# A deeper staging ring for float64 weights, their low parts on VectorE, and queries and keys of eight head pairs turned on TensorE

## The chip, the cores and the metric

The kernel runs as one program on 1 core of a Trainium2 chip. The metric is the device time of one execution in microseconds (us). Three runs of the kernel before gave 1021.06, 1022.9 and 1025.08 us; the median is 1022.9 us. A difference of less than about 0.5% (5 us) can't be told from no change here.

## The reference

Three layers follow one another: blockwise causal attention, a two-layer feed-forward block whose weights come as float64, and a soft mixture of experts.

```
q, k, v: 8 batches x 8 heads x 576 x 64
scores = q @ k.T / 8, masked so that block i (64 rows) sees blocks j <= i
x  = softmax(scores) @ v                       -> 4608 tokens x 512
h  = x @ w_in   (512 x 2048, given as float64)
g  = where(h > 0, h, exp(min(h, 0)) - 1)
x  = g @ w_out  (2048 x 512, given as float64)
logits = x @ phi (32 slots);  d = softmax over tokens;  c = softmax over slots
slot_in  = d.T @ x;  slot_out[e] = relu(slot_in[e] @ w1[e]) @ w2[e]
out = c @ slot_out                             -> 4608 x 512, float32
```

## The kernel before, in words

The 64 heads are worked in 32 pairs; pair `n` has batch `n // 4`. The 4608 tokens are worked in 36 tiles of 128. A small planner (`Plan`, `add`, `order`) simulates all operations with rough durations and sorts them by a key; its result is a fixed order of instructions on each engine. The engines then run their lists in order, each instruction waiting for its semaphores. SP issues nearly all DMAs, in order too. Where the planner sees TensorE at rest, it places small bf16 matmuls that nothing reads (L994, here called fillers).

**A pair.** `pair_load` brings q and k of the pair into `RQ` and `RK` (two slots each) with eight DMAs of 72 KB: one for each tensor, head and half of the head's 64 columns. Each reads runs of 32 floats (128 bytes), 576 of them, so that 32 x 32 blocks lie where VectorE's block transpose needs them. `pair_prep` turns q and k with one VectorE transpose each (L452) and scales q on GpSimd (L454). `pair_scores` makes scores (L490, L494), their row maxima on VectorE (L503) and the exponentials on ScalarE (L506). `pair_weights` divides by the sums on GpSimd (L523), transposes the weights on TensorE (through `transpose`, L317) and copies them out of PSUM. `pair_values` multiplies by v (L589, L593).

**The float64 weights.** `w_in` and `w_out` are each read in 16 pieces of 512 KB as pairs of 32-bit words. `narrow` makes float32 of a piece: one rescaling of the high words on ScalarE or GpSimd (L375, L377), then three VectorE operations (L379, and L382 twice), from a raw buffer (`raws`, here five; GT and G are the later buffers of the tiles) into an output buffer (`outs`, here two called narrow and two called wot). `first_weights` then keeps a rounded high part (ScalarE, L392) and the rest, the low part (GpSimd, L393), for each `w_in` piece. `second_weights` stores each narrowed `w_out` piece to DRAM (`wo_f`), transposes it on TensorE (L317) and multiplies it with phi (L411, the projection) into a PSUM bank that `give_back` copies into WP. `w_in` pieces take raw buffers 0 to 4 and outputs 0 to 3 in turn; `w_out` pieces take raw buffers 3 to 5 and only the two narrow outputs, of which each stays occupied until its store to DRAM has landed.

**A tile.** `tile_range` multiplies a tile with a quarter of `w_in` (L626 to L628: high by high, high by low, low by high; four such steps for each quarter), and VectorE applies the activation. The tile is then turned by way of DRAM (`turned`), meets WP (L668) and updates the dispatch sums. Since WP and several buffers of the tiles are taken by the weight conversion, the tiles can't run steadily before the last projection (L411). From there to the tail TensorE works without gaps. The tail computes the experts and the output.

Of the kernel before, what the change touches and what calls it, by code (L numbers as in the profile page):

```python
# [14 lines left out]
AF = mybir.ActivationFunctionType  # L15
# [10 lines left out]
KWIN, KWOUT = -92.0, -42.0  # L26
KWS, KWOS, KA0, KAS, KCON, KLD, KSTAGE, NPB = 3.5, 1.0, -109.0, 14.0, -98.0, 30.0, 26.0, 4
NEV, NQ = 16, 1
TLAG, LATE = 2.5, 30
TICK, DUTY, FILL, FN = 3.4, 0.5, 0.055, 128  # L30
# [170 lines left out]
def attention_moe_kernel(ctx: ExitStack, tc, q, k, v, w_in, w_out, phi, w1, w2, consts, out):  # L201
# [129 lines left out]
    def start():  # L331
# [11 lines left out]
        def zero(e):  # L343
            for s in range(2):
                nc.gpsimd.memset(f(PB + PW[0] * s + S, 64), 0.0)
            for s in range(NV):
# [7 lines left out]
               [(GT + 1024 * j, 512, gtk(j)) for j in range(2)] + \  # L354
               [(XR + 2 * RING + S, RING, [("xr", p, 1, j) for p in (2, 3) for j in range(2)])]
        outs = [(PAD + 512 * j, ("narrow", j)) for j in range(2)] + [(C + 512 * j, ("wot", j)) for j in range(2)]

# [29 lines left out]
        def first_weights(j):  # L387
            r, kk = divmod(j, 4)
            kw = KWIN + KWS * j
            w32, wk = narrow(win32[P * kk:P * kk + P, 1024 * r:1024 * r + 1024], kw, j % 5, j % 4)  # L390
            hi, lo = W[r] + 512 * kk, W[r] + PIECE + 512 * kk
            add("ACT", 0.5, lambda e: nc.scalar.copy(fr(hi, 512), f(w32, 512)), r=[wk], w=[("wh", r, kk)], key=kw)  # L392
            add("POOL", 1.25, lambda e: nc.gpsimd.tensor_tensor(  # L393
                out=fr(lo, 512), in0=f(w32, 512), in1=f(hi, 512), op=ALU.subtract),
                r=[wk, ("wh", r, kk)], w=[("wl", r, kk)], key=kw)

        def second_weights(m):
            kw = KWOUT + KWOS * m
            w32, wk = narrow(wout32[P * m:P * m + P, :], kw, 3 + m % 3, m % 2)
            load(wo_f32[P * m:P * m + P, :], f(w32, 512), 1 << 18, r=[wk], w=[("wod", m)], key=kw)  # L400
# [14 lines left out]
        def give_back():  # L415
            add(CP2, cpdur(512), lambda e: copy(e, f(WP, 512), pb(GTB, 512)), r=["gtb"], w=["wp"], key=KWOUT)
            for j, (_, _, keys) in enumerate(raws):
                handover(keys, [("stage", j)])
            handover(["c"], [("wot", 0), ("wot", 1)])
            handover([("tt", 0, r) for r in range(2)], [("narrow", 0), ("narrow", 1)])  # L420
            handover([("e", 0), ("e", 1)] + [("xr", p, 1, j) for p in range(2) for j in range(2)], [("stage", 5)])
# [7 lines left out]
    def pair_load(n, key):  # L429
        b, p = divmod(n, 4)  # L430
        s = n % 2
        for src, base, nm in ((q, RQ, "rq"), (k, RK, "rk")):
            for a in range(4):
                h, db = 2 * p + a // 2, a % 2
                load(f(base + S * s, S, 32 * a, 32 * a + 32).rearrange("p (t i) -> p t i", i=32),
                     src[b, h, :, 32 * db:32 * db + 32].rearrange("(t j) i -> j t i", j=32), 147456,
                     w=[(nm, s, a)], key=key, eng=queue(n))
# [10 lines left out]
    def pair_prep(n, key):  # L448

        s = n % 2  # L450
        for src, t, nm, td in ((RQ + S * s, QT + S * s, "rq", ("qt", s)), (RK + S * s, KT + S * s, "rk", ("kt", s))):
            add("DVE", 0.77, lambda e, t=t, src=src: nc.vector.transpose(out=f(t, S), in_=f(src, S)),  # L452
                r=[(nm, s, a) for a in range(4)], w=[td], key=key)
# [518 lines left out]
    for n in range(NPAIR):  # L972
        b, p = divmod(n, 4)
        base = T * 4.5 * (b - 1) + 24.0 * p - 24.0 if b else KAS * p + KA0
        ev.append((base - KLD, lambda n=n, x=base - KLD: pair_load(n, x)))
        ev.append((base - 14, lambda n=n, x=base - 14: pair_prep(n, x)))
# [52 lines left out]
```

## Time and profile before

| | |
|---|---|
| median of three runs | 1022.9 us |
| profiled execution | 1022.02 us |
| its span | 1020.2 us |
| TensorE busy | 969.3 us (95%) |
| VectorE busy | 641.6 us (63%) |
| ScalarE busy | 470.1 us (46%) |
| GpSimd busy | 277.9 us (27%) |
| last projection L411 | starts at 145.42 us |

The profiled execution lasted 1.8 us longer than its span of records. A share of busy time over the whole span mixes three stages: the start, in which the weights are converted beside the first pairs; the long middle, in which tiles and pairs alternate; and the tail. The stage tables of the trace (busy time of each engine in a stretch, granted TensorE clock, share of the DMA engines) tell them apart.

### The profile page before, as it was taken

The page shows a single profiled execution, that of the slowest core. Times are in us where ns is not written, and L with a number is a line of the kernel's source. Part 1 is how long each engine was busy: PE and PEld are TensorE (multiplying, and loading weights), DVE is VectorE, ACT ScalarE, POOL GpSimd, SP SyncE. Part 2 cuts the span into 40 slices and gives each one's busy share as a digit, 9 for nine tenths or more (in the row PEclk, how much of TensorE's full clock was granted, in tenths as well). Part 3 has the DMA queues.
Part 4 walks back from the last instruction along what each step waited for, and adds up shares of the span by engine and source line. Part 5 has one row for each costly group of instructions (what it writes and reads, how often), then busy time and mean ns, then how long its engine had stood idle before and what let it go on. Part 6 is the DMA issues. An engine that isn't in the chain of part 4 may idle for free.

```text
span 1020.2 us, 19113 instructions
## 1 busy us (share of the span) xinstructions
PE 969.3 (95%) x6878; PEld 649.4 (64%) x6878; DVE 641.6 (63%) x1596; ACT 470.1 (46%) x1309; POOL 277.9 (27%) x397
## 2 busy tenths in 40 slices
PE   7779889999999999999999999999999999999993
PEld 5546676666666666666666666666666667776351
DVE  6998655666656667576777676766777664443151
ACT  3765425555554545454444444454444443232134
POOL 3886302222231323222323222322232221100000
PEclk9989879999999999999999999999999999999996
DMA  9988855454545454544445445444543239238969
GB/s 170 222 189 208 192 166 131 120 126 128 139 117 128 119 130 127 130 122 116 122 126 134 118 127 141 127 111 119 133 109 115 88 103 393 100 124 296 354 233 354
DMA packets 262685, 160.85 MB, mean 158 GB/s; under 512 B 197312, under 2 KB 228160, under 8 KB 262592
## 3 DMA queue, kind: packets, MB, share of 16 engines
q1 hardware_dynamic: 260816, 159.43, 56.0%
q8 instruction: 54, 0.88, 0.4%
q10 hardware_dynamic: 1776, 0.22, 0.2%
q14 instruction: 39, 0.32, 0.1%
HBM read 114.51 MB, written 45.09 MB: 156 GB/s over the span
## 4 chain that ended last, share of the span: by engine, by line
PE 82%; DMA 7%; DVE 4%; POOL 2%; ACT 2%; issue 1%; SPq 1%; ACTq 0%; DVEq 0%; POOLq 0%
PE ps L626 15%; PE ps L628 13%; PE ps L627 13%; PE ps L317 10%; PE ps L593 7%; PE ps L494 7%; PE ps L724 4%; PE ps L490 3%; PE ps L668 3%; DMA wo_f<-g 2%; POOL att L523 1%; DMA att<-in_moe_w_dram 1%; DMA g<-in_moe_w_in_dram 1%; DVE g L382 1%; PE ps L895 1%
## 5 line engine op out<-in xcount | busy, mean ns | idle before, releaser
L626 PE MATMUL ps<-w,xhl 128*128 128x512 f32 x576 | 252.2, 438 | 1.7 <-DVE g L636 1.7
L523 POOL TENSOR_SCALAR att<-att,base 128x128 f32<-128x128 f32 (+4 forms) x288 | 173.8, 621 | 220.7 <-DVE base L519 168.8
L628 PE MATMUL ps<-w,xhl 128*128 128x512 f32 x576 | 227.0, 394 | 0.0
L627 PE MATMUL ps<-w,xhl 128*128 128x512 f32 x576 | 226.2, 393 | 0.0
L506 ACT ACTIVATE att<-ps,base 128x128 f32<-128x128 f32 (+4 forms) x288 | 157.6, 553 | 114.9 <-DVE base L503 113.3
L293 ACT COPY att<-ps 128x512 f32<-128x512 f32 (+3 forms) x241 | 112.5, 511 | 113.2 <-PE ps L317 109.2
L626 PEld LDWEIGHTS ps<-w,xhl 128*128 128x128 f32 x576 | 109.0, 189 | 62.8 <-issue 37.2
L503 DVE TENSOR_REDUCE base<-ps 128x1 f32<-128x128 f32 (+4 forms) x288 | 137.5, 503 | 16.9 <-ACT att L506 13.7
L631 ACT ACTIVATE xe<-ps 128x512 f32<-128x512 f32 x144 | 86.1, 598 | 112.9 <-PE ps L628 111.3
L633 DVE TENSOR_SCALAR xe<-xe 128x512 f32<-128x512 f32 x144 | 67.8, 471 | 103.3 <-ACT xe L631 102.6
L317 PE MATMUL ps<-base,att 128*128 128x128 f32 x800 | 117.9, 281 | 13.7 <-POOL att L523 9.0
L628 PEld LDWEIGHTS ps<-w,xhl 128*128 128x128 f32 x576 | 108.4, 188 | 25.0
L317 PEld LDWEIGHTS ps<-base,att 128*128 128x128 f32 x800 | 91.8, 143 | 44.5 <-POOL att L523 22.9
L627 PEld LDWEIGHTS ps<-w,xhl 128*128 128x128 f32 x576 | 109.3, 190 | 13.2
L494 PE MATMUL ps<-att 64*128 64x128 f32 (+3 forms) x512 | 99.0, 477 | 2.8 <-ACT att L506 2.8
L636 DVE TENSOR_TENSOR g<-xe,ps 128x512 f32<-128x512 f32 x144 | 97.5, 677 | 2.6
L613 POOL TENSOR_TENSOR xhl<-xe,xhl 128x512 fp32r<-128x512 f32 x36 | 47.5, 1321 | 183.5 <-ACT xhl L611 130.6
L593 PE MATMUL ps<-att 128*64 128x512 f32 (+4 forms) x640 | 88.3, 422 | 0.0
L644 DVE STREAM_TRANSPOSE g<-g 128x512 f32<-128x512 f32 x120 | 82.5, 688 | 3.5 <-PE ps L317 2.7
L454 POOL TENSOR_SCALAR att<-att 128x576 f32<-128x576 f32 x32 | 22.9, 716 | 192.1 <-DVE att L452 164.1
L593 PEld LDWEIGHTS ps<-att 128*64 128x64 f32 x640 | 43.2, 137 | 42.4 <-issue 33.2
L494 PEld LDWEIGHTS ps<-att 64*128 64x128 f32 x512 | 43.0, 188 | 39.8 <-issue 15.1
(122 smaller groups left out, 1074.0 us busy)
## 6 DMA issues: line engine op xcount, KB each, us to landing
turned<-g SPq DMA_DIRECT2D x60, 512.0 KB, 2.7
g<-turned SPq DMA_DIRECT2D x240, 128.0 KB, 3.1
att<-in_moe_w_dram SPq DMA_DIRECT2D x11, 1024.0 KB, 12.8
att<-in_k_dram SPq DMA_DIRECT2D x127, 72.0 KB, 2.9
att<-in_q_dram SPq DMA_DIRECT2D x126, 72.0 KB, 2.6
att<-in_v_dram SPq DMA_DIRECT2D x64, 128.0 KB, 2.9
g<-in_moe_w_in_dram SPq DMA_DIRECT2D x16, 512.0 KB, 6.0
w_late<-in_moe_w_dram SPq DMA_DIRECT2D x8, 1024.0 KB, 6.5
```

What stands on the lines that cost most here:

```text
L293: nc.scalar.copy(o, i)
L317: mm(o, lhsT=i, rhs=f(IDN + base, n, base, base + n), start=True, stop=True, is_transpose=True)
L494: mm(pb(at((u, h)), P * (u + 1)), lhsT=f(qt + P * u, P, 64 * h, 64 * h + 64), rhs=f(kt, P * (u + 1), 64 * h, 64 * h + 64), start=True, sto ...
L503: add("DVE", 0.08 + wide(x) / 960, lambda e, x=x, c=c: nc.vector.tensor_reduce(out=f(c, 1), in_=pb(at(x), wide(x)), axis=AX.X, op=ALU.max, ...
L506: add("ACT", 0.42 + wide(x) / 1300, lambda e, x=x, c=c: nc.scalar.activation(f(pat(x, n), wide(x)), pb(at(x), wide(x)), AF.Exp, bias=f(c, ...
L523: add("POOL", 0.2 + wide(x) / 1050, lambda e, x=x, p=p: nc.gpsimd.tensor_scalar(out=f(p, wide(x)), in0=f(p, wide(x)), scalar1=f(rs_col + 9 ...
L593: mm(pb(PVB + q0 - 64, S - q0, 64 * h, 64 * h + 64), lhsT=f(vs + 320 * h + D * c, D), rhs=f(pts[h] + CHS * c + q0, S - q0), start=(c == 0) ...
L626: mm(pb(bank, 512), lhsT=fr(xh + P * kk, P), rhs=hi, start=(kk == 0), stop=False)
L627: mm(pb(bank, 512), lhsT=fr(xh + P * kk, P), rhs=lo, start=False, stop=False)
L628: mm(pb(bank, 512), lhsT=fr(xl + P * kk, P), rhs=hi, start=False, stop=(kk == 3))
L631: add("ACT", 0.48, lambda e: nc.scalar.activation(f(ee, 512), pb(bank, 512), AF.Exp), r=[("h", hb)], w=[("e", hb)], key=kr)
L636: add("DVE", 0.6, lambda e: nc.vector.tensor_tensor(out=f(g, 512), in0=f(ee, 512), in1=pb(bank, 512), op=ALU.max), r=[("e", hb), ("h", hb) ...
```

## The change

- The number of raw buffers rises from five to seven in the list (a new one over g slots 6 and 7); `w_in` pieces use six in turn (0, 1, 2, 3, 4, 6) and `w_out` pieces four (3, 4, 6, 5).
- Narrow outputs rise from two to four; the two wot buffers come after them. `w_in` pieces use all six in turn, `w_out` pieces the four narrow ones.
- The low part of `w_in` is subtracted on VectorE, no longer on GpSimd (16 operations of 128 x 512).
- For pairs 0 to 7 q and k are loaded by two DMAs each, one for each head: 96 partitions hold six tokens each, in runs of 64 floats (256 bytes), into a ring of three buffers that lies over RQ and RK. TensorE turns them in two groups of three transposes for each tensor, all through the PSUM area PVB; after each group ScalarE copies it out in token order, scaling q on the way. Pairs 8 to 31 are as before, and wait for the ring of three to be given back.
- The constants (with the identity that a TensorE transpose needs) are loaded first. The planner's figure for a q or k DMA of pairs 8 to 31 rises, and the loads of pairs 0 to 7 are entered 27 instead of 30 key units ahead.

```diff
-KWS, KWOS, KA0, KAS, KCON, KLD, KSTAGE, NPB = 3.5, 1.0, -109.0, 14.0, -98.0, 30.0, 26.0, 4
+KWS, KWOS, KA0, KAS, KCON, KLD, KSTAGE, NPB = 3.5, 1.0, -109.0, 14.0, -150.0, 30.0, 26.0, 4
-TLAG, LATE = 2.5, 30
+TLAG, LATE, NTP = 2.5, 30, 8
...
-               [(XR + 2 * RING + S, RING, [("xr", p, 1, j) for p in (2, 3) for j in range(2)])]
-        outs = [(PAD + 512 * j, ("narrow", j)) for j in range(2)] + [(C + 512 * j, ("wot", j)) for j in range(2)]
+               [(XR + 2 * RING + S, RING, [("xr", p, 1, j) for p in (2, 3) for j in range(2)]),
+                (G + 3072, 512, [("g", 6), ("g", 7)])]
+        outs = [(PAD + 512 * j, ("narrow", j)) for j in range(4)] + [(C + 512 * j, ("wot", j)) for j in range(2)]
...
-            w32, wk = narrow(win32[P * kk:P * kk + P, 1024 * r:1024 * r + 1024], kw, j % 5, j % 4)
+            w32, wk = narrow(win32[P * kk:P * kk + P, 1024 * r:1024 * r + 1024], kw, (0, 1, 2, 3, 4, 6)[j % 6], j % 6)
...
-            add("POOL", 1.25, lambda e: nc.gpsimd.tensor_tensor(
+            add("DVE", 0.6, lambda e: nc.vector.tensor_tensor(
                 out=fr(lo, 512), in0=f(w32, 512), in1=f(hi, 512), op=ALU.subtract),
...
-            w32, wk = narrow(wout32[P * m:P * m + P, :], kw, 3 + m % 3, m % 2)
+            w32, wk = narrow(wout32[P * m:P * m + P, :], kw, (3, 4, 6, 5)[m % 4], m % 4)
...
+        if n < NTP:
+            for j, src in enumerate((q, k)):
+                x = (2 * n + j) % 3
+                for h in range(2):
+                    load(f(RQ + 768 * x, 768, 0, 96).rearrange("p (t y) -> p t y", t=6)[:, :, D * h:D * h + D],
+                         src[b, 2 * p + h].rearrange("(p t) d -> p t d", t=6), 230000, w=[("raw", x, h)], key=key, eng=queue(n))
+            return
...
-                     src[b, h, :, 32 * db:32 * db + 32].rearrange("(t j) i -> j t i", j=32), 147456,
+                     src[b, h, :, 32 * db:32 * db + 32].rearrange("(t j) i -> j t i", j=32), 340000,
...
+        if n < NTP:
+            for j, (t, td) in enumerate(((QT + S * s, "qt"), (KT + S * s, "kt"))):
+                x = (2 * n + j) % 3
+                for t0 in (0, 3):
+                    def tr(e, x=x, t0=t0):
+                        for y in range(3):
+                            i = f(RQ + 768 * x + P * (t0 + y), P, 0, 96)
+                            mm(pb(PVB + 96 * y, 96), lhsT=i, rhs=f(IDN, 96, 0, 96), start=True, stop=True, is_transpose=True)
+                    add("PE", 0.35, tr, r=[("raw", x, 0), ("raw", x, 1), "con"], w=["pvb"], key=key, load=0.0)
+                    add("ACT", cpdur(288)[0], lambda e, t=t, t0=t0, td=td: nc.scalar.activation(
+                        f(t, S).rearrange("c (p t) -> c t p", t=6)[:, t0:t0 + 3], pb(PVB, 288).rearrange("c (t p) -> c t p", p=96),
+                        AF.Copy, scale=SCALE if td == "qt" else 1.0), r=["pvb"], w=[(td, s)], key=key)
+            return
```

The new order follows from the planner. First place: SP's list at the start of the program. Every row is a DMA with its target and source and the shape at the target; g is the area of the raw buffers. Before:

```order
L312 DMA att<-in_q_dram 32x18x32 x2
L312 DMA att<-in_k_dram 32x18x32 x3
L312 DMA att<-in_v_dram 128x4x64 x2
L312 DMA att<-in_v_dram 64x2x64
L312 DMA att<-in_q_dram 32x18x32 x4
L312 DMA att<-in_k_dram 32x18x32 x4
L312 DMA g<-in_moe_w_in_dram 128x1024 x2
```

With the change:

```order
L312 DMA base<-in_consts_dram 128x291
L312 DMA att<-in_q_dram 96x6x64
L312 DMA att<-in_k_dram 96x6x64
L312 DMA att<-in_v_dram 128x4x64 x2
L312 DMA att<-in_v_dram 64x2x64
L312 DMA att<-in_q_dram 96x6x64 x2
L312 DMA g<-in_moe_w_in_dram 128x1024 x2
```

Ahead of the first two pieces of `w_in` stand 8 DMAs, where there were 16.

Second place: VectorE's list right behind its first clearing operations. The L452 rows turn q and k; after the change L380 and L383 are the old L379 and L382, L525 and L528 the old L500 and L503, and L394 is the subtraction. Before:

```order
L452 STREAM_TRANSPOSE att<-att 128x576 x2
L503 TENSOR_REDUCE base<-ps 128x1
L452 STREAM_TRANSPOSE att<-att 128x576
L500 MEMSET ps 64x64 x2
L503 TENSOR_REDUCE base<-ps 128x1 x2
L452 STREAM_TRANSPOSE att<-att 128x576
L500 MEMSET ps 64x64 x4
```

With the change:

```order
L528 TENSOR_REDUCE base<-ps 128x1
L380 TENSOR_SCALAR g<-g 128x512
L383 SCALAR_TENSOR_TENSOR g<-g 128x512
L525 MEMSET ps 64x64 x2
L383 SCALAR_TENSOR_TENSOR g<-g 128x512
L528 TENSOR_REDUCE base<-ps 128x1 x2
L525 MEMSET ps 64x64 x2
L394 TENSOR_TENSOR w_68<-g,w_68 128x512
```

The transposes are gone; the first weight piece comes ahead of most of pair 0's reductions, and its subtraction stands among them.

Third place: TensorE's list among the projections of `w_out` (L411, after the change L412). The L317 rows that read g are the transposes of `w_out` pieces; L651 to L653 are the old L626 to L628; L470 are the new transposes of q and k. Before:

```order
L626 MATMUL ps<-w_69,xhl 128x512
L627 MATMUL ps<-w_69,xhl 128x512
L628 MATMUL ps<-w_69,xhl 128x512
L411 MATMUL ps<-base 128x32 x4
L317 MATMUL ps<-base,g 128x128 x4
L494 MATMUL ps<-att 128x256 x2
```

With the change:

```order
L412 MATMUL ps<-base 128x32 x4
L317 MATMUL ps<-base,g 128x128 x4
L470 MATMUL ps<-base,att 128x96 x3
L651 MATMUL ps<-w_68,xhl 128x512
L652 MATMUL ps<-w_68,xhl 128x512
L653 MATMUL ps<-w_68,xhl 128x512
```

Groups of three new transposes stand between the projections and the first tile's matmuls. Up to the last projection TensorE has the same rows of scores, values, transposed weights and projections in both lists; the new list has 72 transposes L470 more, 344 fillers instead of 375, and 10 instead of 11 steps of the first tile.

## Rows read from the trace of the kernel before

**Rows 1.** Windows: length, busy us and count by engine, granted clock, DMA share, GB/s.

```profile
core 0: us, PE busy (x) PEld busy (x) DVE busy (x) ACT busy (x) POOL busy (x), PEclk, DMA share, GB/s
0.00:18.00 18.00, 13.14 (x121) 10.15 (x121) 9.88 (x29) 4.23 (x9) 4.96 (x14) 1.00 0.94 165
18.00:76.00 58.00, 43.97 (x354) 29.15 (x356) 53.80 (x111) 39.68 (x111) 48.82 (x52) 0.90 0.93 205
76.00:147.00 71.00, 61.73 (x458) 47.73 (x454) 52.08 (x101) 31.83 (x73) 27.21 (x34) 0.86 0.76 194
...
260.00:360.00 100.00, 100.00 (x678) 66.11 (x677) 64.33 (x171) 50.99 (x151) 28.30 (x44) 1.00 0.51 126
```

**Rows 2.** Chain that ended last, around the last projection: start, us, what.

```profile
136.49 4.10 DMA g<-in_moe_w_out_dram
...
145.42 1.92 PE ps L411 x8
147.34 0.59 PE ps L626
```

**Rows 3.** Waits, 76 to 147 us: in total, times, longest; then SP's.

```profile
ACT g L375 <- DMA g<-in_moe_w_out_dram: 11.0, 5, 3.2
...
DVE g L379 <- DMA wo_f<-g: 9.1, 6, 2.7
...
SPq L312 <- DVE g L382: 25.2, 10, 4.3
```

**Rows 4.** DMA issues of the page: count, KB each, us to landing.

```profile
att<-in_k_dram SPq DMA_DIRECT2D x127, 72.0 KB, 2.9
...
att<-in_v_dram SPq DMA_DIRECT2D x64, 128.0 KB, 2.9
...
wo_f<-g SPq DMA_DIRECT2D x16, 256.0 KB, 4.6
```

**Rows 5.** VectorE groups, 0 to 147 us: busy us, mean ns, idle before.

```profile
L382 DVE SCALAR_TENSOR_TENSOR g<-g 128x512 uint32<-128x512 uint32 x38 | 32.8, 862 | 0.3
...
L382 DVE SCALAR_TENSOR_TENSOR base<-g,base 128x512 uint32<-128x512 uint32 x16 | 15.6, 973 | 0.1
L452 DVE STREAM_TRANSPOSE att<-att 128x576 f32<-128x576 f32 x14 | 10.6, 765 | 5.9 <-DMA att<-in_q_dram 4.8 <-DMA att<-in_k_dram 1.0
...
L382 DVE SCALAR_TENSOR_TENSOR g<-xe,g 128x512 uint32<-128x512 uint32 x10 | 7.6, 757 | 1.1 <-ACT xe L293 0.8
```

**Rows 6.** GpSimd groups, 0 to 147 us.

```profile
L393 POOL TENSOR_TENSOR w<-g,w 128x512 fp32r<-128x512 f32 x8 | 11.5, 1439 | 0.0
L393 POOL TENSOR_TENSOR w<-base,w 128x512 fp32r<-128x512 f32 x8 | 10.9, 1372 | 4.2 <-ACT w L392 4.2
```

**Rows 7.** Timelines of VectorE and GpSimd at 61 to 67 and 82 to 85 us.

```profile
62.05 0.69 DVE L382 SCALAR_TENSOR_TENSOR base<-g,base 128x512 uint32<-128x512 uint32 x1
...
82.44 3.14 DVE L382 SCALAR_TENSOR_TENSOR g<-g 128x512 uint32<-128x512 uint32 x2
...
61.67 5.16 POOL L523 TENSOR_SCALAR att<-att,base 128x384 f32<-128x384 f32 x6 [0.96 <-DVE base L519]
...
83.49 1.54 POOL L393 TENSOR_TENSOR w<-base,w 128x512 fp32r<-128x512 f32 x1
```

**Rows 8.** Timelines of SP and VectorE: first issue of w_in, its first conversion.

```profile
9.94 0.97 SPq L312 DMA_DIRECT2D g<-in_moe_w_in_dram  x2
...
15.99 0.43 DVE L379 TENSOR_SCALAR g<-g 128x512 uint32<-128x512 uint32 x1 [0.38 <-POOL g L377]
```

**Rows 9.** DMA queue, 2 to 9 us: packets, MB, time as share of 16 engines.

```profile
q1 hardware_dynamic: 6333, 0.93, 102.9%
```

**Rows 10.** Windows of the fillers alone (L994).

```profile
0.00:147.00 147.00, 30.37 (x375) 27.26 (x375) 0.90 0.85 195
```

**Rows 11.** Chain in the steady stage: eight TensorE transposes in a row.

```profile
202.93 1.02 PE ps L317 x8
```

**Rows 12.** ScalarE copies of 384 columns out of PSUM, 0 to 147 us.

```profile
L293 ACT COPY att<-ps 128x384 f32<-128x384 f32 x9 | 4.3, 481 | 3.8 <-PE ps L317 3.8
```

More of the change, by code (lines that the diff above doesn't have):

```diff
@@ L419, in give_back @@
             handover(["c"], [("wot", 0), ("wot", 1)])
-            handover([("tt", 0, r) for r in range(2)], [("narrow", 0), ("narrow", 1)])
+            for hf in range(2):
+                handover([("tt", hf, r) for r in range(2)], [("narrow", 2 * hf), ("narrow", 2 * hf + 1)])
             handover([("e", 0), ("e", 1)] + [("xr", p, 1, j) for p in range(2) for j in range(2)], [("stage", 5)])
@@ L431, in pair_load @@
         s = n % 2
+        if n < NTP:
[5 more added lines that the diff above has]
+            return
+        if n == NTP:
+            handover([(nm, y, a) for nm in ("rq", "rk") for y in range(2) for a in range(4)], [("raw", x, h) for x in range(3) for h in range(2)])
         for src, base, nm in ((q, RQ, "rq"), (k, RK, "rk")):
@@ L974, in attention_moe_kernel @@
         base = T * 4.5 * (b - 1) + 24.0 * p - 24.0 if b else KAS * p + KA0
-        ev.append((base - KLD, lambda n=n, x=base - KLD: pair_load(n, x)))
+        ev.append((base - (27 if n < NTP else KLD), lambda n=n, x=base - KLD: pair_load(n, x)))
         ev.append((base - 14, lambda n=n, x=base - 14: pair_prep(n, x)))
```

## The prediction

> **What bounds the kernel now.** I read the stage windows first, since busy shares over the whole span mix stages with different limits. In a steady stretch such as 260 to 360 us TensorE is busy all the time at the full clock [rows 1]; no edit there pays unless it takes work off TensorE. In the three stretches up to 147 us it is not: other engines set the pace. From 18 to 76 us VectorE is busy 53.8 of 58 us and the DMA engines 0.93 of the time. From 76 to 147 us VectorE falls to 52.1 of 71 us and the DMA share to 0.76 [rows 1]: nothing is full, so a chain of waits sets the end. The chain view names it: it runs through a load of a `w_out` piece and its conversion to the last projection at 145.42 us, 1.92 us long, and the first tile's matmuls follow at 147.34 us [rows 2]. The wait view gives the reasons: VectorE waited 9.1 us for stores of earlier pieces (the two narrow outputs), ScalarE 11.0 us for loads (the raw buffers), and SP, which issues in order, stood 25.2 us for VectorE [rows 3]. A store takes 4.6 us to land [rows 4]; a narrow output is thus held for its conversion plus the store, 7 us or so, and two of them give a piece every 3.5 us or slower.
>
> So I split the time in three: the time t0 at which the last projection ends (147.3 us now), the rest of the span after it, 1020.2 - 147.3 = 872.9 us, and the 1.8 us by which the profiled execution is longer than its span. By the order, TensorE has the same work behind that point as before but for a few rows. The change is worth what t0 moves, less what is added behind it.
>
> **The change part by part.**
>
> *Work on VectorE up to t0.* It is 9.9 + 53.8 + 52.1 = 115.8 us now [rows 1]. Fourteen block transposes go: -10.6 us [rows 5]. Sixteen subtractions come. No subtraction of two SBUF operands runs on VectorE before; the nearest row is L382, with two SBUF inputs of the same size and 0.69 us when no GpSimd subtraction runs [rows 7]. Its means with all contention, 0.76 to 0.97 us [rows 5], are the upper bound. I take 0.68: +10.9 us (bounds 10.9 and 15.5).
>
> *What the GpSimd subtractions cost VectorE.* The 64 instructions of L382 took 32.8 + 15.6 + 7.6 = 56.0 us [rows 5]; at 0.68 each they would take 43.5. The excess is 12.5 us. Beside the GpSimd scalings L523 one took 0.69 us; two that ran into a GpSimd subtraction L393 took 3.14 us [rows 7]. The L393 rows last 11.5 + 10.9 = 22.4 us in all [rows 6], and they go. I take 8 of the 12.5 us (bounds 0 and 12.5). The Trainium skill, GPSIMD Engine Reference, section Specifications, says that GpSimd shares its SBUF interfaces with VectorE and that they contend when the VectorE instruction has two SBUF inputs. That speaks against the edit, since the new subtractions are of that kind; the trace agrees beside L393 and disagrees beside L523. By the rule alone the relief would be lost and the subtractions dear, which is rival D below.
>
> VectorE's work is then 115.8 - 10.6 + 10.9 - 8 = 108.1 us.
>
> *VectorE's idle time up to t0* is now 147 - 115.8 = 31.2 us. With four narrow outputs a store has the time of three further pieces to land, 6 us even at 2 us a piece, against 4.6 [rows 4], so the 9.1 us of waits for stores go. At the start `w_in` moves ahead: SP issues it now at 9.94 us and VectorE first touches it at 15.99 us [rows 8]; with 8 instead of 16 DMAs ahead on SP it goes out about 4 us sooner, and VectorE has that work while it waits for pair 0: -4 us. The other waits (for scores, loads and copies) I leave: 31.2 - 9.1 - 4 = 18.1 us. Hence t0 = 108.1 + 18.1 = 126 us. Ends: 114 if the whole excess and all but 10 us of idle time go (115.8 - 10.6 + 10.9 - 12.5 + 10); 141 if loads or contention keep their hold (rivals C and D).
>
> *DMA work up to t0.* It is 0.94 x 18 + 0.93 x 58 + 0.76 x 71 = 125 us of all engines now [rows 1]. By the issue order 72 q and k DMAs of 576 pieces each run up to 130 us, 41,472 pieces of 128 bytes; the new order has 30 of 576 pieces before the last `w_out` load, 17,280 of 256 bytes. If a piece cost by its bytes, about 0.9 MB less would be moved, 4 us at some 200 GB/s. If each piece cost the same, 24,192 of them at 1.029 x 7 us x 16 / 6333 = 18 ns [rows 9] over 16 engines would save 27 us. A v transfer of 128 KB in 256-byte pieces lands as fast as a 72 KB one of q or k in 128-byte pieces [rows 4], so I go near the upper end and take 20: 105 us. At the share of 0.93 that the second stretch shows this needs 113 us, so DMA would not end after VectorE. The Trainium skill, DMA: Bandwidth & Descriptors, section Specifications, puts line rate only at 512 bytes and above; both sizes are below it, and by that alone the saving would be nearer to nothing. The equal landing times speak against it.
>
> *TensorE up to t0.* It is busy 13.1 + 44.0 + 61.7 = 118.8 us [rows 1], of which 30.4 us are fillers [rows 10]; 88.4 us are work. The 72 new transposes before t0 add 72 x 1.02 / 8 = 9.2 us [rows 11] (bound below: 0.75 of that, for 96 instead of 128 columns). 97.6 us fit in 126. ScalarE gets 24 copies of 288 columns, under the 0.48 us of a 384-column copy [rows 12]: 11.5 us on top of 75.7 busy of 147, also covered. Its strided target is not in the trace; at twice the price it would be 23 us, still covered. GpSimd only loses work.
>
> *Behind t0.* Pairs 6 and 7 have 24 transposes there, 24 x 1.02 / 8 = 3.1 us, in a stretch where TensorE has no idle time. One step of the first tile (three matmuls, under 1 us) moves behind t0 too. The block transposes they replace lie on VectorE, 64 of 100 us busy there [rows 1], and give back nothing. Rest: 872.9 + 3.1 + 1 = 877 us. The higher planner figure for later q and k loads reorders the middle; with TensorE full before, I cost it at nothing, and at 0 to 3 us if it opens gaps. The constants come first on SP, which delays pair 0 by one issue; VectorE's earlier `w_in` work hides it.
>
> Sum: 126 + 877 + 1.8 = 1004.8 us against 1022.0 of the profiled execution. The median shown is 0.9 us above that, so I forecast 1005 us.
>
> **The rivals.**
>
> B, a larger gain: t0 = 114, as above, and 993 to 994 us. For it: in the second stretch VectorE stood only 4.2 of 58 us, so it can run dense. Against it: DMA work of 105 us in 114 would have to be nearly gapless.
>
> C, the loads take the place of the stores. ScalarE waited 11.0 us for loads, more than VectorE did for stores [rows 3]. If bytes keep coming at 194 GB/s, the 71 us of the third stretch move 13.8 MB, and shrink only by the q and k no longer fetched there, some 5 us; with 4 us from the start t0 is 138 and the time 1017 us. Against it: the DMA share there is 0.76, so there is room for 255 GB/s.
>
> D, contention stays: no relief, and subtractions at 0.97 us: VectorE's work is 115.8 - 10.6 + 15.5 = 120.7 us, t0 = 139, the time 1018 us. This is the case of the rule on two SBUF inputs.
>
> E, slower: TensorE's new chain takes over the start. It runs in order, and a group of three transposes must wait for its q or k load and for ScalarE's copy of the group before, since all go through one PSUM area; scores and projections queue behind it. Price: 24 groups at 0.38 + 0.48 us is 21 us if nothing lies between, and with three raw buffers instead of four each of six pairs may wait some 5 us for a load: 51 us in all. TensorE has 126 - 97.6 = 28 us to spare, so it decides from there on: t0 = 126 + 51 - 28 = 149, the time 1028 us. For it: TensorE waits in order already now, and GpSimd's weights hold it up. Against it: the planner puts other work between the groups.
>
> That the deeper ring doesn't do what it says would be C; the order keeps each load behind a store on SP, but four pieces back.
>
> **How the numbers follow.** Forecast (997 to 1013 us) 0.53, B 0.14, C 0.14, D 0.10, E 0.09. The range that holds the time 8 times in 10 reaches over most of B's and all of C's and D's times: 989 to 1020 us. About 0.5%, 5 us, can be told from no change. Faster by more than that, below 1017.8 us, takes the forecast, B, and half of C and D: 0.79. Within 0.5% are the other half and a little of E: 0.13. Slower: 0.08.
>
> **What would show it.** Right: the last projection ends near 126 us; VectorE has no waits for `wo_f` stores; the L382 operations average about 0.72 us; the subtractions take about 0.7 us on VectorE; VectorE is over 85% busy up to t0; the stretch behind it is 3 to 5 us longer than 873. Wrong: the projections still pace at over 3.5 us behind loads (C); L382 still at 0.87 us (D); TensorE waiting for q or k loads or for copies out of PVB, with VectorE idle behind it (E); or gaps on TensorE in the middle, which would spoil the sum at a place where I expect nothing.

## The result, and the profile after

Four runs of the changed kernel gave 1009.79 to 1014.45 us, median 1010.73 us; the kernel before gave 1022.6 us beside them. The ratio is 0.9888, 95% interval 0.9856 to 0.9921: faster by 1.1%. The forecast was 1005 us, with a range of 989 to 1020 us. The span of the profiled execution is 1009.7 us, where it was 1020.2.

One correction comes first, since every later number hangs on it. The prediction took the projections to end at 147.3 us in the kernel before [rows 2]. TensorE's timeline of that kernel has one more group of eight behind the first tile's first steps (columns: start, us, engine, line, operation, and in brackets the idle time before it):

```profile
145.42 1.92 PE L411 MATMUL ps<-base 128*128 128x32 f32 x8 [0.73 <-ACT base L293]
...
151.20 0.97 PE L411 MATMUL ps<-base 128*128 128x32 f32 x8
```

So 145.42 us was the 15th of the 16 groups; t0 before is 152.2 us and the rest of the span 868.0 us, where the prediction had 147.3 and 872.9. The sum is the same; the split was wrong by 4.9 us.

The changed kernel's chain of what ended last, around its last projection and at the transposes behind it (columns: start, us, what):

```profile
134.94 0.81 PE ps L412 x8
135.75 0.32 PE ps L651
...
147.02 0.25 PE ps L470 x3
...
148.43 0.34 PE ps L470 x3
```

t0 is now 135.75 us, 16.4 us earlier, and the rest 874.0 us, 5.9 us longer: -16.4 + 5.9 = -10.5 us, the difference of the spans. The pace of the projections (duration min/median/max in ns, first and last start) tells the same. Before, then after:

```profile
L411 PE MATMUL ps<-base x128: 192/276/423, 89.6 to 151.9; 128*128 128x32 f32 x128
```

```profile
L412 PE MATMUL ps<-base x128: 192/276/298, 87.3 to 135.5; 128*128 128x32 f32 x128
```

The 16 pieces of `w_out` begin nearly as early as before and then come every (135.5 - 87.3) / 15 = 3.2 us, where it was 4.2.

The stage windows of the changed kernel, as in [rows 1], with one row for all of t0; below it the same row of the kernel before:

```profile
0.00:18.00 18.00, 14.06 (x121) 10.98 (x121) 5.30 (x16) 8.46 (x16) 1.58 (x10) 1.00 1.01 208
18.00:76.00 58.00, 50.83 (x445) 35.03 (x444) 53.46 (x135) 46.99 (x130) 36.96 (x46) 0.97 0.79 198
76.00:135.75 59.75, 53.67 (x426) 41.89 (x427) 48.76 (x98) 29.72 (x66) 24.16 (x26) 0.97 0.71 220
...
0.00:135.75 135.75, 118.56 (x991) 87.90 (x992) 107.52 (x247) 85.17 (x209) 62.70 (x81) 0.97 0.78 209
...
136.00:1009.70 873.70, 848.28 (x5953) 561.98 (x5951) 525.25 (x1360) 393.74 (x1115) 194.68 (x298) 0.99 0.53 152
```

```profile
0.00:152.15 152.15, 123.99 (x953) 91.42 (x954) 117.07 (x243) 76.32 (x193) 80.98 (x98) 0.89 0.83 190
...
152.20:1020.20 868.00, 845.28 (x5926) 557.91 (x5925) 524.57 (x1353) 393.80 (x1116) 196.91 (x299) 0.99 0.52 152
```

Read the third busy time: VectorE's work up to t0 fell from 117.1 to 107.5 us, its idle time from 35.1 to 28.2. So 9.6 us of the 16.4 look like work and 6.9 like idle time; the experiments show that this reading misleads. Behind t0 TensorE's busy time rose by 3.2 us (848.5 us from 135.75 us on; the row above begins at 136.0) and its idle time by 2.7.

The mean granted clock of TensorE up to t0 rose as well, from 0.89 to 0.97. By itself it isn't the cause: e1 below has nearly the whole gain at 0.91, and e4 has none at 0.96.

VectorE's waits in the changed kernel, 0 to 136 us (in total, times, longest), against the 9.1 us for stores in [rows 3]:

```profile
DVE base L528 <- PE ps L515: 13.0, 2, 11.6
DVE base L295 <- ACT xe L293: 5.7, 1, 5.7
DVE ps L525 <- PE ps L519: 3.0, 3, 1.4
DVE g L380 <- POOL xe L378: 1.5, 1, 1.5
```

No wait for a store of `wo_f` is left. In its place stands one wait of 11.6 us for the first scores. The timeline of the start shows its making, against [rows 8]:

```profile
6.45 1.12 SPq L312 DMA_DIRECT2D g<-in_moe_w_in_dram  x2
...
11.40 0.67 ACT L472 ACTIVATE att<-ps 128x288 f32<-128x288 f32 x1 [0.56 <-PE ps L470]
...
12.13 1.19 PE L515 MATMUL ps<-att 64*64 64x288 f32 x8 [0.54 <-ACT att L472]
...
13.38 0.65 POOL L378 TENSOR_SCALAR g<-g 128x512 f32<-128x512 f32 x1 [11.87 <-DMA g<-in_moe_w_in_dram]
14.04 0.42 DVE L380 TENSOR_SCALAR g<-g 128x512 uint32<-128x512 uint32 x1
```

`w_in` is issued 3.5 us sooner and first converted at 14.04 instead of 15.99 us, but the scores wait for four groups of transposes, each copied out before the next through the one PSUM area.

VectorE's groups up to 136 us, against [rows 5], and those of ScalarE and TensorE that are new:

```profile
L383 DVE SCALAR_TENSOR_TENSOR g<-g 128x512 uint32<-128x512 uint32 x48 | 38.0, 810 | 0.4
...
L394 DVE TENSOR_TENSOR w<-g,w 128x512 fp32r<-128x512 f32 x12 | 8.3, 709 | 0.0
...
L383 DVE SCALAR_TENSOR_TENSOR base<-g,base 128x512 uint32<-128x512 uint32 x8 | 6.0, 748 | 0.0
...
L383 DVE SCALAR_TENSOR_TENSOR g<-xe,g 128x512 uint32<-128x512 uint32 x8 | 5.5, 690 | 0.1
...
L394 DVE TENSOR_TENSOR w<-base,w 128x512 fp32r<-128x512 f32 x4 | 3.0, 754 | 0.0
```

```profile
L472 ACT ACTIVATE att<-ps 128x288 f32<-128x288 f32 x24 | 17.0, 707 | 8.6 <-PE ps L470 8.6
```

```profile
L470 PE MATMUL ps<-base,att 96*128 96x96 f32 x72 | 11.1, 266 | 3.6 <-DMA att<-in_q_dram 3.1 <-ACT att L472 0.5
```

### The profile page after: what moved, and what is told of

The parts are those of the page before. It is cut to its first block, busy times and chain, and to the rows that moved or that the text cites. A ratio compares the mean times of both kernels' runs of the same rounds, so it can differ in the third digit from the quotient of the medians.

```text
span 1009.7 us, 19263 instructions
## 1 busy us (share of the span) xinstructions
PE 967.1 (96%) x6943; PEld 650.1 (64%) x6943; DVE 632.8 (63%) x1607; ACT 479.1 (47%) x1324; POOL 257.4 (25%) x379
## 4 chain that ended last, share of the span: by engine, by line
PE 85%; DMA 5%; DVE 4%; ACT 2%; POOL 1%; issue 1%; SPq 0%; ACTq 0%; DVEq 0%; POOLq 0%
PE ps L651 15%; PE ps L653 13%; PE ps L652 13%; PE ps L317 11%; PE ps L618 8%; PE ps L519 7%; PE ps L749 4%; PE ps L515 3%; PE ps L693 3%; PE ps L1019 1%; DVE g L383 1%; DMA att<-in_q_dram 1%; POOL att L548 1%; DMA att<-in_moe_w_dram 1%; PE ps L920 1%
## 5 line engine op out<-in xcount | busy, mean ns | idle before, releaser
L651 PE MATMUL ps<-w,xhl 128*128 128x512 f32 x576 | 251.3, 436 | 2.4 <-DVE g L661 2.4
L548 POOL TENSOR_SCALAR att<-att,base 128x128 f32<-128x128 f32 (+4 forms) x288 | 175.6, 627 | 254.5 <-DVE base L544 190.1
L653 PE MATMUL ps<-w,xhl 128*128 128x512 f32 x576 | 226.7, 394 | 0.0
L528 DVE TENSOR_REDUCE base<-ps 128x1 f32<-128x128 f32 (+4 forms) x288 | 136.9, 503 | 30.2 <-PE ps L515 15.9
L651 PEld LDWEIGHTS ps<-w,xhl 128*128 128x128 f32 x576 | 108.5, 188 | 61.2 <-issue 36.4
L293 ACT COPY att<-ps 128x512 f32<-128x512 f32 (+3 forms) x231 | 108.8, 514 | 82.0 <-PE ps L317 78.1
L658 DVE TENSOR_SCALAR xe<-xe 128x512 f32<-128x512 f32 x144 | 64.6, 449 | 114.0 <-ACT xe L656 113.2
L317 PE MATMUL ps<-base,att 128*128 128x128 f32 x800 | 117.4, 278 | 9.3 <-POOL att L548 8.2
L653 PEld LDWEIGHTS ps<-w,xhl 128*128 128x128 f32 x576 | 108.1, 188 | 25.0
L317 PEld LDWEIGHTS ps<-base,att 128*128 128x128 f32 x800 | 90.8, 142 | 42.1 <-POOL att L548 18.8
L519 PE MATMUL ps<-att 64*128 64x128 f32 (+3 forms) x512 | 96.5, 469 | 0.0
L638 POOL TENSOR_TENSOR xhl<-xe,xhl 128x512 fp32r<-128x512 f32 x36 | 48.2, 1338 | 168.4 <-ACT xhl L636 137.1
L618 PE MATMUL ps<-att 128*64 128x512 f32 (+4 forms) x640 | 89.6, 427 | 0.0
L618 PEld LDWEIGHTS ps<-att 128*64 128x64 f32 x640 | 43.7, 139 | 43.3 <-issue 34.1
L531 ACT ACTIVATION_READ_ACCUMULATOR att<-ps,base 128x1 f32 x288 | 58.5, 203 | 0.0
```

Of the source, the lines that this page charges most:

```text
L293: nc.scalar.copy(o, i)
L317: mm(o, lhsT=i, rhs=f(IDN + base, n, base, base + n), start=True, stop=True, is_transpose=True)
L519: mm(pb(at((u, h)), P * (u + 1)), lhsT=f(qt + P * u, P, 64 * h, 64 * h + 64), rhs=f(kt, P * (u + 1), 64 * h, 64 * h + 64), start=True, sto ...
L528: add("DVE", 0.08 + wide(x) / 960, lambda e, x=x, c=c: nc.vector.tensor_reduce(out=f(c, 1), in_=pb(at(x), wide(x)), axis=AX.X, op=ALU.max, ...
L531: add("ACT", 0.42 + wide(x) / 1300, lambda e, x=x, c=c: nc.scalar.activation(f(pat(x, n), wide(x)), pb(at(x), wide(x)), AF.Exp, bias=f(c, ...
L548: add("POOL", 0.2 + wide(x) / 1050, lambda e, x=x, p=p: nc.gpsimd.tensor_scalar(out=f(p, wide(x)), in0=f(p, wide(x)), scalar1=f(rs_col + 9 ...
```

## Experiments

Each row is one kernel: its median, its ratio to the kernel before with the 95% interval, and, from its one profiled execution, t0, VectorE's work and idle time up to it, and the rest of the span.

| kernel | median us | ratio | t0 | work | idle | rest |
|---|---|---|---|---|---|---|
| before | 1022.6 | 1 | 152.2 | 117.1 | 35.1 | 868.0 |
| changed | 1010.7 | 0.9888 [0.9856, 0.9921] | 135.8 | 107.5 | 28.2 | 874.0 |
| e1 rings | 1012.7 | 0.9907 [0.9873, 0.9941] | 140.0 | 117.0 | 23.0 | 869.4 |
| e2 subtractions | 1031.5 | 1.0091 [1.0072, 1.0109] | 157.8 | 119.2 | 38.6 | 871.7 |
| e3 turn | 1032.0 | 1.0088 [1.0064, 1.0112] | 153.7 | 105.9 | 47.8 | 876.9 |
| e4 rings, subtractions | 1024.2 | 1.0033 [1.0014, 1.0052] | 152.3 | 115.9 | 36.4 | 870.3 |
| e5 turn, rings | 1014.4 | 0.9928 [0.9907, 0.9949] | 136.1 | 103.3 | 32.8 | 877.5 |
| e9 subtractions, turn | 1024.7 | 1.0028 [1.0005, 1.0050] | 157.0 | 104.4 | 52.6 | 872.5 |
| e6 subtractions back, same order | 1021.7 | 1.0013 [0.9990, 1.0037] | 145.8 | 104.0 | 41.8 | 874.2 |
| e7 planner's figures | 1019.5 | 0.9979 [0.9955, 1.0002] | 141.5 | 107.4 | 34.1 | 877.0 |
| e8 four v buffers | 1011.9 | 0.9916 [0.9886, 0.9946] | 135.4 | 103.1 | 32.3 | 877.1 |
| e10 pair 0 the old way | 1010.0 | 0.9876 [0.9855, 0.9898] | 136.4 | 108.2 | 28.2 | 872.6 |
| e11 six pairs | 1010.6 | 0.9874 [0.9841, 0.9908] | 142.4 | 107.4 | 35.0 | 872.0 |
| e12 pairs 1 to 5 | 1010.3 | 0.9899 [0.9866, 0.9932] | 136.1 | 107.1 | 29.0 | 870.6 |

The profiled executions of e9 and e11 were the longest of their kernels, 6.6 and 5.6 us over the median; the others lay within 2.4 us of it. Each ratio is to the kernel before as it ran beside that kernel: 1021.5 us for e1 to e8, 1021.7 for e9 to e11, 1020.6 for e12. Differences between kernels below are differences of medians; the gains and losses of a part alone are to 1021.5 us.

### The three parts one by one: e1, e2, e3

Each is the kernel before with one part of the change. The rings are one part here: e1 deepens the raw buffers and the narrow outputs together. The planner makes a new order for each.

```diff
 e1: rings only
-        outs = [(PAD + 512 * j, ("narrow", j)) for j in range(2)] + ...
+        outs = [(PAD + 512 * j, ("narrow", j)) for j in range(4)] + ...
...
 e2: subtractions only
-            add("POOL", 1.25, lambda e: nc.gpsimd.tensor_tensor(
+            add("DVE", 0.6, lambda e: nc.vector.tensor_tensor(
 e3: the changed kernel with the old rings, and the subtractions on GpSimd
+            ... kw, j % 5, (0, 1, 4, 5)[j % 4])
+            ... kw, 3 + m % 3, m % 2)
```

> Only the deeper rings (raw buffers and narrow outputs), on the kernel before; subtractions stay on GpSimd, q and k as before. Theory A (the stores of the narrowed w_out pieces held the loop; the rings are the larger part of the gain): VectorE's 9.1 us of waits for stores vanish, the last projection ends 8 to 10 us sooner, about 1013 us. Theory B (the loads were just as late, the gain comes from turning q and k on TensorE): waits move from the stores to the loads, 1019 to 1022 us.

> Only the 16 low-part subtractions moved to VectorE, on the kernel before. Theory A: VectorE takes 10.9 us more and gets back about 8 of contention, in a stage where it is nearly full: no change, 1021 to 1026 us. Theory B: the same, but as GpSimd's time matters too (it was 8.7 of 10 us busy there), up to 5 us faster, 1018 us.

> Only the new way of q and k for pairs 0 to 7 (with the constants first), rings and subtractions as in the kernel before. Theory A: VectorE's start comes 4 us later (first scores at 12 instead of 8 us) and the store waits stay; 10.6 us of VectorE work go: 3 to 5 us faster at most, 1018 to 1022 us. Theory B: most of the gain is here, 1012 to 1014 us.

The rings alone give 0.9907, nearly the whole gain; the other two alone cost 0.9% each. e1's window up to its t0:

```profile
0.00:140.00 140.00, 118.43 (x938) 89.04 (x939) 117.00 (x244) 77.14 (x195) 78.73 (x97) 0.91 0.85 211
```

VectorE has the same work as before, 117.0 against 117.1 us, and 12.1 us less idle time; no wait for a store is listed. That is the forecast's mechanism of the rings by itself. It is not all due to the narrow outputs, though: SP's waits for conversions to free a raw buffer fell as well, from 31.4 to 18.7 us up to t0, and the two rings were not tried apart.

e3 is the warning. The turning takes VectorE's work down by 11.2 us, as forecast, and t0 doesn't move:

```profile
0.00:153.70 153.70, 128.39 (x993) 96.93 (x994) 105.85 (x232) 87.85 (x214) 74.31 (x91) 0.89 0.70 183
```

The idle time grew by 12.7 us. VectorE's waits for stores of `wo_f` are only 4.2 us here. Up to 136 us SP stood 41.4 us for conversions to free a raw buffer, where it was 29.4 in the kernel before:

```profile
SPq L312 <- DVE g L383: 41.4, 15, 11.1
```

TensorE waited 12.2 us for GpSimd's scalings, no longer than in the kernel before (13.1 us up to its t0).

### Two parts at a time: e4, e5, e9

```diff
 e4: rings and subtractions, no pair turned on TensorE
-TLAG, LATE, NTP = 2.5, 30, 8
+TLAG, LATE, NTP = 2.5, 30, 0
 e5: rings and turning, subtractions on GpSimd, planned anew
-            add("DVE", 0.6, lambda e: nc.vector.tensor_tensor(
+            add("POOL", 1.25, lambda e: nc.gpsimd.tensor_tensor(
 e9: subtractions and turning, old rings
+            ... kw, j % 5, (0, 1, 4, 5)[j % 4])
+            ... kw, 3 + m % 3, m % 2)
```

> Rings and subtractions of the changed kernel, q and k turned on VectorE as before. Theory A: as the rings alone, 1011 to 1014 us, first scores at 8 us again, so near the changed kernel. Theory B: 1018 to 1021 us.

> The changed kernel with its subtractions on GpSimd again, the planner knowing it. If the three parts work through VectorE's load (theory A, as corrected by the first four runs: the rings take the store waits away, and VectorE then has no room for the subtractions unless its block transposes go), then without the subtractions VectorE has more room still: 1004 to 1010 us. If the subtractions help by freeing VectorE from GpSimd's contention (theory C): 1015 to 1018 us, L383 near 0.87 us.

> The changed kernel with the rings of the kernel before (five raw buffers, two narrow outputs for w_out): subtractions on VectorE and q and k turned on TensorE. Theory A (the rings are the part without which nothing is gained): at or above the time of the kernel before, 1020 to 1030 us, with VectorE waiting 5 us or more for stores again. Rival (turning and subtractions together are a gain of their own): 1014 to 1018 us.

The rings gain in every company: 9 us alone, 7 beside the subtractions (e2 to e4), 18 beside the turning (e3 to e5), 14 beside both (e9 to the changed kernel). The other two don't. The subtractions cost 10 us alone and 12 beside the rings (e1 to e4), and gain 7 beside the turning (e3 to e9) and 4 beside both (e5 to the changed kernel). The turning costs 10 alone and 2 beside the rings (e1 to e5), and gains 7 beside the subtractions (e2 to e9) and 14 beside both (e4 to the changed kernel). Each pays only with the other: together, on top of the rings, they are worth 2 us, and the intervals of e1 and of the changed kernel overlap over most of their length.

One caution: e4 keeps what comes with the turning, the constants first and the planner's higher figure for q and k loads, and that figure now holds for all pairs. Its planner placed 670 fillers up to t0, where e1 has 357 up to 140 us. So the differences that have e4 at one end are not one part alone.

What the rings do in every company can be read from the pace of the projections (in e9, then in e4):

```profile
L412 PE MATMUL ps<-base x128: 190/276/422, 90.5 to 156.7; 128*128 128x32 f32 x128
```

```profile
L412 PE MATMUL ps<-base x128: 193/277/298, 104.5 to 152.0; 128*128 128x32 f32 x128
```

From the first start to the last, the 16 groups take 59.3 to 66.2 us in the four kernels with the old rings (the kernel before, e2, e3, e9) and 41.3 to 52.8 us in the ten with the deeper ones. e4 has this pace too, 47.5 us; it is late because its projections begin at 104.5 us, where e1's begin at 88.1.

### The subtractions in the same order: e6

Every replanned kernel differs in its order as well. e6 keeps the changed kernel's order to the last row: the planner still sees a VectorE operation, and only the engine that is issued to is another.

```diff
-            add("DVE", 0.6, lambda e: nc.vector.tensor_tensor(
+            add("DVE", 0.6, lambda e: nc.gpsimd.tensor_tensor(
```

> The changed kernel, each engine's list in the very same order, only that the 16 subtractions are issued on GpSimd at the places they had. No replanning, so it shows what the move itself is worth. Theory A: VectorE loses 11 us of work and gets 8 back as contention: the last projection within 2 us of the changed kernel, 1008 to 1013 us. Theory C (contention and GpSimd's time decide): 1014 to 1020 us.

It lost the whole gain, 11 us, though VectorE is spared 11.3 us of subtractions. Contention takes more than half of these back. Up to t0 both kernels have the same 231 other operations on VectorE; with the subtractions on GpSimd the 64 of L383 take 51.5 us, against 49.5, and the 32 of L380 take 18.8, against 14.9. VectorE's work falls by 3.5 us only, and t0 still comes 10 us later: what grew is its idle time, by 13.6 us. GpSimd's own time is behind that. e6, windows, then what VectorE waited for in 18 to 76 us, then TensorE in 0 to 146 us:

```profile
18.00:76.00 58.00, 48.23 (x389) 33.15 (x388) 43.59 (x110) 41.58 (x113) 47.78 (x55) 0.91 0.75 191
```

```profile
DVE ps L525 <- PE ps L519: 4.5, 3, 3.0
DVE base L528 <- PE ps L515: 3.1, 1, 3.1
DVE base L543 <- ACT att L531: 3.0, 1, 3.0
DVE ps L525 <- ACT att L531: 2.3, 1, 2.3
```

```profile
PE ps L317 <- POOL att L548: 13.2, 13, 2.5
```

The same two lists in the changed kernel:

```profile
DVE ps L525 <- PE ps L519: 1.6, 2, 1.1
DVE base L528 <- PE ps L515: 1.4, 1, 1.4
```

```profile
PE ps L317 <- POOL att L548: 8.2, 14, 1.1
```

GpSimd is busy 47.8 instead of 37.0 of those 58 us. VectorE is busy 43.6 instead of 53.5; the 14 subtractions that it had in this stretch are 9.9 us, the whole difference, and all of it became idle time. GpSimd's scalings of the weights (L548) come later behind the subtractions (L394), TensorE waits longer for them (13.2 against 8.2 us up to t0), and VectorE waits longer for scores and exponentials. The chain of what ended last runs through GpSimd's list, in e6 with subtractions in it, up to VectorE's first copy of a transposed `w_out` piece (L295). e6, then the changed kernel:

```profile
81.41 1.40 POOL w L394
82.81 0.83 POOL att L548
83.64 1.67 POOL w L394
85.31 4.15 POOL att L548 x4
...
96.61 0.06 DVE base L295
```

```profile
74.69 5.62 POOL att L548 x5
...
86.54 0.07 DVE base L295
```

At L295 e6 is 10 us late, and at t0 still 10 us: its projections begin at 97.4 instead of 87.3 us and then keep the same pace (48.1 and 48.2 us from first to last). In this order, by one profile of each kernel, the subtractions' place matters through GpSimd's queue; what VectorE is spared is not what decides.

### The start: e7, e10

The first scores come 4.4 us later than before. e7 tells the planner the measured price of the new operations; e10 loads and turns pair 0 the old way, into a buffer of its own.

```diff
 e7
-                    add("PE", 0.35, tr, ...
-                    add("ACT", cpdur(288)[0], ...
+                    add("PE", 0.45, tr, ...
+                    add("ACT", 0.7, ...
 e10
-        if n < NTP:
+        if 0 < n < NTP:
...
+                 if n else ((q, PT + 2 * PTW, "rq0"), (k, PT + 2 * PTW + S, "rk0")):
```

> The changed kernel, but the planner is told what the new operations took in the trace: 0.7 us for ScalarE's strided copy instead of 0.29, and 0.45 instead of 0.35 us for three transposes. VectorE's list then begins with the first w_in piece and not with pair 0's maximum, for which it stood 11.6 us. Theory D (the late start is what the forecast missed): VectorE's idle time in the first 18 us falls from 12.7 to about 9 us, 1005 to 1008 us. Rival (the start is made up for later, as SP and the loads set the pace from 60 us on): 1009 to 1013 us.

> The changed kernel, but pair 0 alone is loaded in 128-byte runs into other buffers and turned on VectorE as before. Theory D (the late start is a loss that stays): first scores at 8 instead of 12 us, VectorE's idle time in the first 18 us 8 instead of 12.7 us, the last projection some 4 us sooner, 1005 to 1008 us. Rival (a new plan moves waits about by as much as that, or the lost time is given back behind): 1008 to 1016 us, with no relation between the first scores and the last projection.

e7 was slower than the changed kernel by 9 us, with truer figures, and VectorE still sat idle for 12.3 of the first 18 us. A new order alone can thus cost several us, for reasons that are not in the planner's figures. e10 did what it should at the start and nothing for the time:

```profile
0.00:18.00 18.00, 13.07 (x108) 10.12 (x109) 9.56 (x30) 7.02 (x16) 5.50 (x14) 0.97 1.11 194
18.00:76.00 58.00, 47.73 (x417) 32.38 (x415) 48.14 (x118) 44.57 (x122) 39.09 (x43) 0.95 0.77 199
```

VectorE's idle time in the first 18 us fell from 12.7 to 8.4 us, and rose in the next 58 from 4.5 to 9.9. t0 is 136.4, and 1010.0 us isn't told from 1010.7. In this kernel, planned anew, the late start costs nothing that isn't lost later anyway.

### The raw buffers in the middle, and the work behind t0: e8, e11, e12

From 60 to 80 us the DMA share falls to 0.32, and SP waits 16.5 us up to t0 for values (L618) to free a v buffer. e8 gives v a fourth buffer. e11 turns six pairs instead of eight, which takes the 24 transposes behind t0 away; e12 joins e10 and e11.

```diff
 e8
-    NV = 3
+    NV = 4
 e11
-TLAG, LATE, NTP = 2.5, 30, 8
+TLAG, LATE, NTP = 2.5, 30, 6
```

> The changed kernel with four instead of three buffers for v. SP stood 16.5 us behind v loads that waited for TensorE to finish an earlier pair's product with v, 11.0 us at one stretch (62 to 74 us), and the w_out loads stood behind them. Theory E (that stretch costs the time): the wait goes, DMA share in 60 to 80 us rises from 0.32 to over 0.6, the last projection 5 to 9 us sooner, 1002 to 1006 us. Rival (w_out buffers are full by then anyway, VectorE is what is late): 1008 to 1012 us.

> The changed kernel with six instead of eight pairs turned on TensorE; pairs 6 and 7, whose transposes fall into the stretch where TensorE is full, are turned on VectorE. If the 24 transposes cost what a row of eight showed (0.128 us each, 3.1 us) and little else: the time from the last projection to the end falls from 874 to about 871 us, the whole to 1006 to 1009 us. Rival (TensorE hides them in waits that stay anyway): 1009 to 1012 us and no shorter rest.

> The two last edits together: of the changed kernel only pairs 1 to 5 are turned on TensorE, pair 0 and pairs 6 and 7 on VectorE. Neither edit alone changed the time by more than its interval. If the rest behind the last projection is shorter by the 24 transposes (2 to 3 us, as with six pairs) and the early first scores are worth nothing: 1007 to 1010 us. If the order that the planner makes is what decides at this size: anywhere from 1005 to 1016 us, and the last projection moves by more than the rest does.

e8's waits of SP, and the window:

```profile
SPq L313 <- DVE g L384: 25.0, 18, 4.4
...
SPq L313 <- PE ps L619: 9.6, 2, 8.1
```

```profile
60.00:80.00 20.00, 15.09 (x131) 10.00 (x131) 17.95 (x43) 13.38 (x36) 16.89 (x17) 1.00 0.30 94
```

SP's wait for values fell from 16.5 to 9.6 us, with one of 8.1 us still in 55 to 85 us, and its wait for conversions rose from 18.7 to 25.0. The DMA share was 0.30, and t0 135.4: the fourth buffer didn't take the wait away, and VectorE was busy 18.0 of the 20 us. In e11 and e12 the rest is 872.0 and 870.6 us, 2.0 and 3.4 less than 874.0, near the 3.1 us of 24 transposes; but kernels that keep these transposes spread over 5 us there, and the medians can't tell it. No version beats the changed kernel by what can be measured.

## Why the prediction was right, and where it was not

**The stores: right.** With the deeper rings the waits for stores are gone, and e1 shows that the rings alone are worth most of the time: 12.1 us of VectorE's idle time with the same work. That the narrow outputs rather than the raw buffers do it is argued from the 9.1 us of waits, not shown.

**VectorE's work: right in sum, in part by luck.** 107.5 us against 108.1. The subtractions took 11.3 us (10.9 forecast), at 0.71 and 0.75 us each (0.68). The operations L382, now L383, went from 56.0 to 49.5 us, 6.5 where 8 were taken (0.77 us each; 8 us would be 0.75, not the 0.72 of the list of signs). L379, now L380, went from 17.7 to 14.9 us, a relief that the forecast had at nothing. Against the kernels that differ by the subtractions and their order, without turning, the relief is 6.8 (49.2 us in e2) and 7.9 (57.0 in e1, 49.1 in e4), but in the same order with turning only 2.0 (e6); and e3, which keeps the subtractions on GpSimd, has 49.3 us as well. So the forecast's reason, that the relief comes because the L393 rows go, accounts for a part of it at most; the new order gives the rest. The rule of the Trainium skill, GPSIMD Engine Reference, section Specifications, that two SBUF inputs on VectorE contend with GpSimd, gave rival D; the new subtractions, which have two such inputs, are not dear beside GpSimd's scalings (the one at 45.02 us took 0.68 us with scalings L548 running all the while), and D fell.

**VectorE's idle time: the step that failed.** "The other waits (for scores, loads and copies) I leave: 31.2 - 9.1 - 4 = 18.1 us" gave t0 = 126; it was 28.2 us, and t0 = 135.8. Of these 10.1 us, 3.9 come from the misread end, since up to the true t0 the idle time before was 35.1 us, not 31.2; it fell by 6.9 us where 13.1 were forecast. VectorE is busy 79% of the time up to t0, not over 85%, and rival B with its t0 of 114 is far off. Two things are wrong with it. The start didn't save 4 us; it cost 4.6 (12.7 us idle in the first 18, 8.1 before), since the first scores wait for the chain of transposes and copies. That was rival E's mechanism, at one place only; in all TensorE waited 3.1 us for q loads and 1 us for copies, so E as a whole fell. With the 9.1 us of stores gone, these 4.6 leave 2.4 us that went elsewhere. The deeper fault is that idle times were subtracted one from another as if each were on the path. e10 mended the start and the idle time came up elsewhere; e3 took 11.2 us of work away and got 12.7 us of idle time. Up to t0 VectorE isn't the engine that sets the pace in all companies: work of 103.1 to 108.2 us (e5, e8, e10, e12, the changed kernel) ends at the same 135.4 to 136.4 us, and e1's 117.0 at 140.0.

**"GpSimd only loses work": the wrong value for a right edit.** The subtractions' move was priced as VectorE's contention, which in the same order gives back 6 to 8 of the 11.3 us (6.3 by the durations of L383, L380 and L543, 7.7 by VectorE's busy time). e6 shows that the move is worth 11 us in this order all the same, and its chain leads through GpSimd's queue, to TensorE, and back to VectorE. Missed as well: without the turning the move costs time (e2 and e4 are slower than what they are built on). Both were planned anew, and which of order and edit did it isn't told apart.

**DMA work: right.** 0.78 x 135.75 = 106 us against 105 forecast, from 0.83 x 152.15 = 126; e3, with the old rings, has 0.70 x 153.7 = 108, so the new way of q and k gives most of it. As forecast it didn't end last: the share in the last stretch is 0.71.

**ScalarE's copies: mis-sized.** They were put "under the 0.48 us of a 384-column copy"; they took 0.71 us, 17.0 us instead of 11.5, inside the doubled bound. ScalarE is busy 85 of 136 us; where the copies show is the start.

**Behind t0: nearly right.** 874.0 - 868.0 = 5.9 us against 4.1: 3.2 us of busy time on TensorE (the 24 transposes were put at 3.1), and 2.7 us of gaps, in the 0 to 3 us kept for the new order. The kernels that turn pairs 6 and 7 on TensorE have 872.5 to 877.5 us there; the one before, e1, e2 and e4, which turn none, have 868.0 to 871.7.

**C, the loads:** the pace of 3.2 us a piece is under the 3.5 that would have shown it. GpSimd does wait for loads of `w_out` (16.7 us in 76 to 136), and one load of `w_out` lies on the chain of what ended last (7.5 us from 95.92 us on), but SP waits for VectorE to free their buffers.

**The sum.** t0 came 9.8 us later than forecast and the rest was 3.0 us shorter: together 6.7 us, and 1009.7 instead of 1003 us of span. The misread split adds 4.9 us to the one and takes them from the other. Without it t0 moved by 16.4 us where 21.3 were forecast, and the rest grew by 5.9 where 4.1 were.

**What stays open.** Which wait holds t0 at about 136 us in five kernels with different work on VectorE is not settled; neither four v buffers nor an earlier start moved it. It is no fixed pace from a fixed start either: in the five the projections begin between 84.7 and 94.5 us. Raw buffers and narrow outputs were not deepened apart. Nor is it settled how much of the differences among replanned kernels is the order rather than the edit; e6 alone holds the order still.

## What to carry to other kernels

When a change bundles edits, look for the one that lifts a wait by itself (here the deeper rings): it gains in every company, while edits that shift work between engines gain or lose by what else is in the bundle. Work taken off a busy engine is time only if what it waits for is not late too; before adding idle times up, ask what will be late next, the queue of the relieved engine included. And where a planner sets the order, test an edit once with the order held fixed, or its price can't be told from the order's.

## What the runs showed of the hardware

- A ScalarE copy of 128 x 288 out of PSUM into a target with a stride of six floats took 707 ns, longer than a plain one of 128 x 384 at 481 [rows 12]. The scaling in it and the stride were not separated.
- VectorE's operations with a single SBUF input were slower too with the subtractions on GpSimd: in the same order, L380 from g to g took 602 ns on the mean in e6 and 495 in the changed kernel (24 each), and from g to base 634 and 415 (4 each).
- Reading q and k in runs of 256 bytes instead of 128 took the DMA work up to t0 from 126 us to 106, for nearly the same bytes (190 GB/s x 152.15 us = 28.9 MB, 209 x 135.75 = 28.4); in e3, which has the old rings, to 108. The Trainium skill, DMA: Bandwidth & Descriptors, section Specifications, puts line rate at 512 bytes and more. Below it the 20 us saved here are nearer to a price by the piece (27 us in the prediction) than to one by the byte (4 us).
